# Sliding-window attention and SwiGLU on one core: the last third of the output weights queued ahead of the second tile's values, the fourth tile's values loaded one attention step later

## The chip, the cores and the metric

The kernel runs on one core of a Trainium2 chip. The metric is the device time of one execution in microseconds (us), lower is better. Three executions of the kernel before took 330.44, 330.54 and 331.67 us, median 330.54.

## The reference, cut to what matters

```python
# q, k, v: (8 batches, 8 heads, 576 positions, 64); window = 64
scores = (q @ k.T) / sqrt(64)                  # per batch and head
mask   = (0 <= i - j) & (i - j < 64)           # causal, 64 wide
attn   = softmax(where(mask, scores, -1e9)) @ v
x      = attn, heads side by side               # (4608 tokens, 512)
out    = (silu(x @ w_gate) * (x @ w_val)) @ w_out   # 512 -> 1536 -> 512
```

All inputs and the output are float32; the kernel computes in bfloat16 with float32 sums.

## The kernel before, in words

The 4608 tokens are worked through as nine tiles of 512 tokens, `t` = 0 to 8. Tiles 0 to 6 and 8 are the first 512 positions of one batch each; tile 7 (`LAST`) gathers the last 64 positions of all eight batches. Counted from one, "the second tile" is t = 1 and "the fourth tile" is t = 3.

Each tile passes three stages on TensorE (PE):

- **attention**: `scores` (L261), an exponential on ScalarE (ACT), a mask product and a sum on VectorE (DVE, L277 and L282), `totals` (L294), and `mix`, the product with the values (L347). DVE scales the result into `xT` (L359).
- **gate and value**: `gate_value` (L398 to L405) for each of twelve blocks `m` of 128 of the 1536 inner columns: four matmuls with `wg`, four with `wv` (all L401), a SiLU on ACT (L394), and a product on DVE into `hT` (L395). PE's two kinds of result tile, `g_ps` and `v_ps`, have two buffers each, so block m + 2 can't start on its value tile before DVE has read that of block m.
- **projection**: `project` and `project_part` (L410), twelve matmuls with `wo` for each of four row groups of the tile; `project_end` copies a row group to `os_` and SyncE (SP) writes it out (L420, L429).

The order on every engine is written out by hand (`manual_schedule`); each engine works through its own instructions in order and waits on semaphores. The projection of tile t - 1 is laid between the attention steps of tile t (L652 to L666), then the gate blocks of tile t follow (L682). In the first round this is the prologue L638 to L650: `scores(1, ...)`, and `columns(c0, c1)`, which projects tile 0 column by column: `columns(7, 10)` uses columns 7, 8 and 9 of `wo`, and `mix_all(1)` comes right after it.

While the gate blocks run, DVE also turns the queries and keys of the next tile (`turn`, L198 and L208), after blocks 4, 6, 8, 10 for t = 1 and 1, 4, 7, 10 later (L681).

**The loads.** GpSimd (POOL) issues the loads that change float32 to bfloat16 on the way: the weights `wg`, `wv`, `wo`, the queries `q_s` (four transfers for a tile, L88), the keys `k_s` (sixteen, L108), and the values of tiles 1 and 2, which go straight into `vb[1]` and `vb[0]` (`load_halves`, eight transfers, one for each head, L137). `wo` comes in three transfers of four columns each (`weights_o`, L178): columns 0 to 3, 4 to 7, 8 to 11. Each transfer that POOL issues signals one of eight semaphores in turn, and an issue waits until the transfer eight places before it has landed. So POOL never has more than eight in flight.

From t = 3 on the values go another way. `stage_v(t)` (L155) has SP load them as float32 into `v_f`, a tile with one buffer, in eight transfers (L137); `cast_v(t)` (L159) has POOL change them to bfloat16 in `vb[t % 2]` with four CASTs (L162). In round t the order is `cast_v(t + 1)`, `load_qk(t + 2)`, `stage_v(t + 2)` (L667 to L675); in round 1 `cast_v` is left out. So in the kernel before the values of tile 3 are staged in round 1, behind the four writes of tile 0's output on SP, and cast in round 2. POOL's CASTs and its DMA issues stand in one order: what is queued behind a waiting CAST waits with it. In round 2 these are the loads of q and k of tile 4, and of `k_l` (L677, sixteen transfers for tile 7).

The two places that the change touches are L561 to L565 (the order of `wo` and `vb[1]` on POOL) and L672 to L675 (the place of `stage_v(3)` on SP).

Of the kernel before, what the change touches and what calls it, by code (L numbers as in the profile page):

```python
# [17 lines left out]
def kernel(  # L18
# [15 lines left out]
    LAST = NT - 2  # L34
# [27 lines left out]
    def batch(t):  # L62
        return t if t < LAST else t - 1
# [38 lines left out]
    def load_k(k_s, groups):  # L102

        w = 4 * D - 32
        for a, c in quarters:
            p0 = 64 * a + 32 * c
            for g, (b, s) in enumerate(groups):
                nc.gpsimd.dma_start(  # L108
                    k_s[p0:p0 + 32, g, :, 0:w],
                    k[b, a:H:2, s:s + P].rearrange("u (r e) d -> r u (e d)", e=4)  # L110
                    [:, :, 32 * c:32 * c + w],
                )
        return k_s

    def load_qk(t):
        q_s = load_q(t)
        if t == 1:
            staged[t] = q_s, None
            return
        if t == LAST:  # L120
            groups = [(b, S - P) for b in range(4)]
        else:
            groups = [(batch(t), P * g) for g in range(4)]
        k_s = stage.tile([P, 4, 4, 4 * D], BF16, name="k_s", tag="k")
        staged[t] = q_s, load_k(k_s, groups)
# [7 lines left out]
    def load_halves(eng, dst, t):  # L133

        for hd in range(H):
            w, x, h = hd // 4, hd // 2 % 2, hd % 2
            eng.dma_start(  # L137
                dst[64 * x:64 * x + 64, :, w, h],
                v[batch(t), hd, 0:512].rearrange("(j r) d -> r j d", r=64),
            )  # L140

    def load_last_v():
        for c in range(2):
            for hd in range(H):
                w, x, h = hd // 4, hd // 2 % 2, hd % 2
                s0 = S - P + 64 * c
                nc.gpsimd.dma_start(
                    vl[64 * x:64 * x + 64, :, c, w, h],
                    v[:, hd, s0:s0 + 64].rearrange("b r d -> r b d"),
                )  # L150

    def new_v(t):
        staged[t, "v"] = stage.tile([P, 8, 2, 2, D], FP32, name="v_f", tag="v", bufs=1)

    def stage_v(t):  # L155
        new_v(t)
        load_halves(nc.sync, staged[t, "v"], t)

    def cast_v(t):  # L159
        for i in range(4):  # L160
            js = slice(2 * i, 2 * i + 2)
            nc.gpsimd.tensor_copy(vb[t % 2][:, js], staged[t, "v"][:, js])  # L162
# [14 lines left out]
    def weights_o(c0, c1):  # L177
        nc.gpsimd.dma_start(  # L178
            wo[:, c0:c1, :],
            moe_w_out[P * c0:P * c1].rearrange("(c r) f -> r c f", r=P),  # L180
        )
# [21 lines left out]
    def turn(t, u):  # L203
        turn_q(t, u)
        turn_k(kT[t % 2], staged[t][1], u)

    def turn_k(dst, k_s, u):
        nc.vector.transpose(  # L208
            dst[:, u, :].rearrange("r (g x e) -> r g e x", g=4, e=4),
            k_s[:, :, u].rearrange("r g (e d) -> r g e d", d=D)[:, :, :, 0:32],  # L210
        )
# [97 lines left out]
    def sums(t, w):  # L309
        d = d_tile(), d_tile()  # L310
        totals(t, w, d)
        for x in range(2):
            r = room(1)[:, 0]
            log(r, d[x])
            invert(r)
            inverse[t, 2 * w + x] = r
# [54 lines left out]
    def mix_all(t):  # L371
        tiles = wide("ao_ps"), wide("ao_ps")
        for w in range(2):
            mix(t, w, (tiles[w][:, 0], tiles[w][:, 1]))
        for u in range(4):
            scale(t, u, tiles[u // 2][:, u % 2])
# [20 lines left out]
    def gate_value(t, m):  # L397
        pair = gate_tiles()  # L398
        for ps, w in zip(pair, (wg, wv)):
            for c in range(4):  # L400
                nc.tensor.matmul(  # L401
                    ps[:], w[:, c, P * m:P * m + P], xT[t][:, c, :],
                    start=(c == 0), stop=(c == 3),
                )
        gate_end(t, m, pair)  # L405

    def project_part(t, ss, tiles, cs):
        for c in cs:
            for s, o_ps in zip(ss, tiles):
                nc.tensor.matmul(  # L410
                    o_ps[:], hT[t][:, c, P * s:P * s + P], wo[:, c, :],
                    start=(c == 0), stop=(c == 11),
                )

    def project_end(t, s, o_ps, copy=nc.vector.tensor_copy):
        os_ = fsb.tile([P, 512], FP32, name="os_", tag="os_", bufs=4)
        copy(os_[:], o_ps[:])
        rows = out[S * batch(t):S * batch(t) + 512]
        if t < TURNED:
            nc.sync.dma_start(rows.rearrange("(r e) f -> e r f", e=4)[s], os_[:])  # L420
            return
        if t == LAST:
            rows = out.rearrange("(b s) f -> b s f", s=S)[:, 512:S]
            rows = rows.rearrange("b (r e) f -> e b r f", e=16)
        else:
            rows = rows.rearrange("(r e) f -> e r f", e=16)
        for i in range(4):
            eng = nc.scalar if t == NT - 1 and i % 2 else nc.sync
            eng.dma_start(rows[4 * s + i], os_[32 * i:32 * i + 32])  # L429

    def out_tile():
        return ps_f.tile([P, 512], FP32, name="o_ps", tag="g")

    def project(t, s):
        o_ps = out_tile()
        project_part(t, (s,), (o_ps,), range(12))
        project_end(t, s, o_ps)
# [17 lines left out]
    def set_exp():  # L455
        nc.scalar.preload_act_table_set("natural_log_exp_and_others")  # L456

    def set_silu():
        nc.scalar.preload_act_table_set("silu_and_others")
# [101 lines left out]
    load_qk(1)  # L561
    weights_o(0, 4)
    weights_o(4, 8)
    load_halves(nc.gpsimd, vb[1], 1)
    weights_o(8, 12)  # L565
    for i in range(2):
        on_v(v1[:, i], v_first[:, i])
    scores_first(2)
# [83 lines left out]
    for t in range(1, NT):  # L652
        if t > 1:
            set_exp()
            scores(t, 0)
            project(t - 1, 0)
            o_ps = out_tile()
            project_part(t - 1, (1,), (o_ps,), range(5))
            scores(t, 1)
            sums(t, 0)  # L660
            project_part(t - 1, (1,), (o_ps,), range(5, 12))
            project_end(t - 1, 1, o_ps)
            project(t - 1, 2)
            sums(t, 1)
            mix_all(t)
            project(t - 1, 3)  # L666
        set_silu()  # L667
        if t + 1 == LAST:
            load_last_v()
        elif t + 1 < NT and t > 1:  # L670
            cast_v(t + 1)
        if t + 2 < NT:  # L672
            load_qk(t + 2)
            if t + 2 != LAST:
                stage_v(t + 2)  # L675
        if t == 2:
            k_l = load_k(  # L677
                cast.tile([P, 4, 4, 4 * D], BF16, name="k_l", tag="c0"),
                [(b, S - P) for b in range(4, 8)],
            )  # L680
        turns = (4, 6, 8, 10) if t == 1 else (1, 4, 7, 10)  # L681
        for m in range(12):  # L682
            gate_value(t, m)
            if m in turns and t + 1 < NT:
                turn(t + 1, turns.index(m))
            if m == 8 and 3 <= t < 7:
                turn_k(kT[2], k_l, t - 3)
# [32 lines left out]
```

## Time and profile before

| what | value |
|---|---|
| median of three executions | 330.54 us |
| the profiled execution's own time | 330.49 us |
| its span, first to last instruction | 328.5 us, so 2.0 us lie around the span |
| mean granted TensorE clock | 0.997 |
| PE busy | 319.1 us, 97% of the span |
| DVE, ACT, POOL busy | 220.7, 167.1, 143.5 us |
| POOL's DMA queue | 57.3% of 16 engines over the span |
| SP's DMA queue | 18.7% of 16 engines over the span |

The times in the views are us from the start of the span unless marked ns. A line of the timeline gives start, duration, engine, source line, operation, the tiles written and read, and how many instructions are merged in it; in brackets stands the idle time of the engine before it and what ended that time. A matmul's duration overlaps the next one's, so the time that PE loses at a wait is read from start to start. The view of DMA issues, asked for a stretch that holds one issue, gives the time from that issue to its landing; it has this for POOL's transfers and not for SP's.

### The profile page before, as it was taken

The numbers are of one execution on the slowest core, as the hardware profiler recorded it, in microseconds if no ns is written. First come the engines' busy times: TensorE is split into PE (matmuls) and PEld (weight loads), VectorE is DVE, ScalarE is ACT, GpSimd is POOL, SyncE is SP. The second block draws the span as 40 slices with busy tenths as digits, with TensorE's granted clock in tenths as the row PEclk, the third lists the DMA queues.
The fourth block names the chain that finished last, engine by engine and source line by source line (L and its number), as shares of the span: only waits on it lengthen the run. The fifth ranks groups of instructions, "written<-read, shape, count | busy, mean of one in ns | idle before, by whom it ended". The sixth has DMA issues, their size and how long they took to land.

```text
span 328.5 us, 7003 instructions
## 1 busy us (share of the span) xinstructions
PE 319.1 (97%) x2743; PEld 151.3 (46%) x2743; DVE 220.7 (67%) x352; ACT 167.1 (51%) x239; POOL 143.5 (44%) x256
## 2 busy tenths in 40 slices
PE   7899999989999999999999999999999999999995
PEld 4444434434444444445444544444444544444443
DVE  4865755497857776787668766976787576773431
ACT  4854556336833583357435653566347633773300
POOL 4953465778857935246123899464200000000000
PEclk9999999999999999999999999999999999999998
DMA  7999999999899799329821999899401300020013
GB/s 250 201 201 201 204 148 208 231 199 131 141 238 184 88 208 185 68 42 216 173 65 16 145 190 98 57 177 198 110 3 34 98 0 2 12 87 32 2 34 96
DMA packets 82865, 40.84 MB, mean 124 GB/s; under 512 B 64272, under 2 KB 78352, under 8 KB 82832
## 3 DMA queue, kind: packets, MB, share of 16 engines
q0 software_dynamic: 50672, 23.08, 57.3%
q1 hardware_dynamic: 31136, 16.26, 18.7%
q10 hardware_dynamic: 1024, 1.05, 1.1%
q8 instruction: 21, 0.34, 0.4%
q14 instruction: 12, 0.10, 0.1%
HBM read 54.00 MB, written 9.44 MB: 193 GB/s over the span
## 4 chain that ended last, share of the span: by engine, by line
PE 85%; DMA 8%; DVE 2%; issue 2%; ACT 1%; POOL 1%; SPq 0%; DVEq 0%; POOLq 0%
PE g_ps L401 26%; PE v_ps L401 26%; PE o_ps L410 25%; DMA k_s<-in_k_dram 3%; DMA q_s<-in_q_dram 2%; PE s_ps L261 2%; DMA v_f<-in_v_dram 2%; PE ao_ps L347 2%; PE d_ps L294 1%; DMA k_f<-in_k_dram 1%; PE o_ps L446 1%; PE g_ps L381 1%; PE v_ps L381 1%; ACT L456 0%; PE ao_ps L330 0%
## 5 line engine op out<-in xcount | busy, mean ns | idle before, releaser
L394 ACT ACTIVATE sg<-g_ps 128x512 f32<-128x512 f32 x108 | 64.4, 597 | 115.1 <-PE g_ps L401 87.5
L395 DVE TENSOR_TENSOR hT<-sg,v_ps 128x512 bf16<-128x512 f32 x108 | 74.6, 692 | 59.4 <-PE v_ps L401 57.1
L401 PE MATMUL v_ps<-xT,wv 128*128 128x512 bf16 x424 | 108.8, 379 | 1.0 <-DVE hT L395 1.0
L401 PE MATMUL g_ps<-xT,wg 128*128 128x512 bf16 x424 | 108.8, 379 | 0.1
L410 PE MATMUL o_ps<-wo,hT 128*128 128x512 bf16 x420 | 95.3, 380 | 0.8 <-DMA wo<-in_moe_w_out_dram 0.8
L108 POOL DMA_DIRECT2D k_s<-in_k_dram x112 | 60.4, 551 | 25.0 <-DMA q_s<-in_q_dram 14.8
L401 PEld LDWEIGHTS <-wv 128*128 128x128 bf16 x424 | 41.5, 98 | 51.2 <-issue 1.3
L401 PEld LDWEIGHTS <-wg 128*128 128x128 bf16 x424 | 41.3, 98 | 49.5 <-issue 0.6
L410 PEld LDWEIGHTS <-hT 128*128 128x128 bf16 x420 | 39.1, 98 | 47.5 <-issue 2.9
L274 ACT ACTIVATE eb<-s_ps 128x960 bf16<-128x960 f32 (+1 forms) x32 | 29.5, 974 | 16.3 <-PE s_ps L261 16.2
L208 DVE STREAM_TRANSPOSE kT<-k_s 128x512 bf16<-128x512 bf16 x28 | 35.9, 1284 | 2.0 <-issue 2.0
L277 DVE TENSOR_TENSOR eb<-eb,mask 128x960 bf16<-128x960 bf16 (+1 forms) x32 | 21.6, 675 | 14.3 <-ACT eb L274 14.2
L359 DVE TENSOR_TENSOR xT<-ao_ps,r 128x512 bf16<-128x512 f32 x36 | 23.0, 685 | 7.2 <-PE ao_ps L347 5.6
L162 POOL CAST vb<-v_f 128x512 bf16<-128x512 f32 x20 | 11.9, 644 | 29.7 <-DMA v_f<-in_v_dram 21.6
L304 ACT ACTIVATE r<-d_ps 128x512 f32<-128x512 f32 (+1 forms) x33 | 20.8, 629 | 6.0 <-PE d_ps L294 5.9
L198 DVE STREAM_TRANSPOSE qT<-q_s 128x512 bf16<-128x512 bf16 x32 | 22.4, 702 | 0.6 <-DMA q_s<-in_q_dram 0.6
L307 ACT ACTIVATE r<-r 128x512 f32<-128x512 f32 (+1 forms) x33 | 22.0, 669 | 1.0
L88 POOL DMA_DIRECT2D q_s<-in_q_dram x28 | 15.2, 551 | 16.4 <-DVE qT L198 10.2
L282 DVE TENSOR_TENSOR both<-eb 128x512 bf16<-128x512 bf16 x32 | 13.9, 434 | 1.1
L137 POOL DMA_DIRECT2D vb<-in_v_dram x16 | 10.9, 689 | 7.9 <-DMA wo<-in_moe_w_out_dram 3.8
L456 ACT ACT_TABLE_LOAD x9 | 11.5, 1283 | 2.0 <-issue 1.9
L95 POOL DMA_DIRECT2D q_s<-in_q_dram x16 | 8.6, 598 | 7.8 <-DVE qT L198 6.8
(107 smaller groups left out, 186.8 us busy)
## 6 DMA issues: line engine op xcount, KB each, us to landing
q_s<-in_q_dram POOLq DMA_DIRECT2D x28, 248.0 KB, 6.3
k_s<-in_k_dram POOLq DMA_DIRECT2D x112, 56.0 KB, 4.5
v_f<-in_v_dram SPq DMA_DIRECT2D x40, 128.0 KB
wo<-in_moe_w_out_dram POOLq DMA_DIRECT2D x3, 512.0 KB, 11.1
q_f<-in_q_dram SPq DMA_DIRECT2D x4, 256.0 KB
vb<-in_v_dram POOLq DMA_DIRECT2D x16, 64.0 KB, 5.7
v<-in_v_dram POOLq DMA_DIRECT2D x16, 64.0 KB, 3.1
q_s<-in_q_dram POOLq DMA_DIRECT2D x16, 62.0 KB, 4.0
```

Source lines behind the costliest of these rows:

```text
L108: nc.gpsimd.dma_start(k_s[p0:p0 + 32, g, :, 0:w], k[b, a:H:2, s:s + P].rearrange("u (r e) d -> r u (e d)", e=4) [:, :, 32 * c:32 * c + w],)
L198: nc.vector.transpose(queries[t][:, u, :].rearrange("r (e x) -> r e x", e=16), staged[t][0][:, u].rearrange("r (e d) -> r e d", d=D)[:, :, ...
L208: nc.vector.transpose(dst[:, u, :].rearrange("r (g x e) -> r g e x", g=4, e=4), k_s[:, :, u].rearrange("r g (e d) -> r g e d", d=D)[:, :, ...
L274: nc.scalar.activation(flat, s_ps[h][:].rearrange("r a b -> r (a b)")[:, 0:n], AF.Exp, scale=0.125)
L277: nc.vector.tensor_mul(flat, flat, mask[:].rearrange("r j c e y -> r (j c e y)")[:, 0:n])
L304: nc.scalar.activation(r, d_ps, AF.Ln)
L307: nc.scalar.activation(r, r, AF.Exp, scale=-1.0)
L359: nc.vector.tensor_mul(xT[t][:, u, :], o_ps, inverse.pop((t, u)))
L394: nc.scalar.activation(sg[:], g_ps[:], AF.Silu)
L395: nc.vector.tensor_mul(hT[t][:, m, :], sg[:], v_ps[:])
L401: nc.tensor.matmul(ps[:], w[:, c, P * m:P * m + P], xT[t][:, c, :], start=(c == 0), stop=(c == 3),)
L410: nc.tensor.matmul(o_ps[:], hT[t][:, c, P * s:P * s + P], wo[:, c, :], start=(c == 0), stop=(c == 11),)
```

## The change

Two moves; nothing is added and nothing is taken away. The third transfer of `wo` is issued by POOL ahead of the eight transfers of `vb[1]`, not behind them. The eight transfers of `stage_v(3)` are issued by SP in round 2, after the write of row group 0 of tile 1's output, and no longer in round 1 behind tile 0's output.

```diff
     load_qk(1)
     weights_o(0, 4)
     weights_o(4, 8)
+    weights_o(8, 12)
     load_halves(nc.gpsimd, vb[1], 1)
-    weights_o(8, 12)
     for i in range(2):
         on_v(v1[:, i], v_first[:, i])
...
             set_exp()
             scores(t, 0)
             project(t - 1, 0)
+            if t == 2:
+                stage_v(3)
             o_ps = out_tile()
             project_part(t - 1, (1,), (o_ps,), range(5))
...
         if t + 2 < NT:
             load_qk(t + 2)
-            if t + 2 != LAST:
+            if t > 1 and t + 2 != LAST:
                 stage_v(t + 2)
```

On PE, DVE, ACT the order of instructions stays as it was. On POOL one transfer changes its place among nine; on SP the eight transfers of `v_f` move behind the four writes of `os_` of row group 0 of tile 1.

## The prediction

> **What bounds the kernel now.** I read the page first: engine shares, and in its groups the idle time before each matmul.
>
> ```profile
> PE 319.1 (97%) x2743; PEld 151.3 (46%) x2743; DVE 220.7 (67%) x352; ACT 167.1 (51%) x239; POOL 143.5 (44%) x256
> ...
> L401 PE MATMUL v_ps<-xT,wv 128*128 128x512 bf16 x424 | 108.8, 379 | 1.0 <-DVE hT L395 1.0
> ...
> L410 PE MATMUL o_ps<-wo,hT 128*128 128x512 bf16 x420 | 95.3, 380 | 0.8 <-DMA wo<-in_moe_w_out_dram 0.8
> ```
>
> PE is the bound, and once the pipeline is full the big matmuls wait twice, once each: for `wo` and for `hT`. PE's timeline says where and how long.
>
> ```profile
> 47.72 1.04 PE L410 MATMUL o_ps<-wo,hT 128*128 128x512 bf16 x4
> 49.56 1.89 PE L410 MATMUL o_ps<-wo,hT 128*128 128x512 bf16 x8 [0.80 <-DMA wo<-in_moe_w_out_dram]
> 51.37 1.04 PE L347 MATMUL ao_ps<-eb,vb 64*64 64x128 bf16 x64
> ...
> 66.35 1.03 PE L401 MATMUL g_ps<-xT,wg 128*128 128x512 bf16 x4
> 68.38 1.02 PE L401 MATMUL v_ps<-xT,wv 128*128 128x512 bf16 x4 [1.00 <-DVE hT L395]
> ```
>
> The bracket understates the loss, because a matmul's duration overlaps the next one's. Four matmuls take 1.04 us and one 0.38, so they start (1.04 - 0.38) / 3 = 0.22 us apart. After the four at 47.72 the next was due at 47.72 + 4 x 0.216 = 48.59; it came at 49.56, **0.97 us** late. After the four at 66.35 the next was due at 67.22; it came at 68.38, **1.16 us** late. The table of stretches, cut from gate start to gate start, confirms the second (columns: stretch, its length, then busy time of each engine).
>
> ```profile
> 54.27:89.33 35.06, 34.06 (x281) 15.89 (x281) 25.74 (x38) 19.27 (x28) 29.15 (x51) 1.00 1.22 180
> 89.33:123.22 33.89, 33.89 (x281) 15.86 (x280) 24.19 (x36) 17.97 (x27) 22.98 (x43) 1.00 1.14 180
> ```
>
> The round with the wait is 35.06 - 33.89 = 1.17 us longer than the next, which PE fills wholly. So 0.97 + 1.16 = 2.13 us can be had, no more: the later rounds have no wait to take.
>
> What ends the two waits is read from the timelines of POOL, SP and DVE.
>
> ```profile
> 31.41 0.70 POOL L137 DMA_DIRECT2D vb<-in_v_dram  x1 [0.57 <-DMA wg<-in_moe_w_gate_dram]
> ...
> 42.80 0.68 POOL L137 DMA_DIRECT2D vb<-in_v_dram  x1 [1.98 <-DMA wo<-in_moe_w_out_dram]
> 43.47 0.77 POOL L178 DMA_DIRECT2D wo<-in_moe_w_out_dram  x1
> ...
> 60.55 0.55 POOL L108 DMA_DIRECT2D k_s<-in_k_dram  x1 [0.73 <-DMA k_s<-in_k_dram]
> ```
>
> ```profile
> 57.15 7.68 SPq L137 DMA_DIRECT2D v_f<-in_v_dram  x8
> ```
>
> ```profile
> 66.50 1.31 DVE L208 STREAM_TRANSPOSE kT<-k_s 128x512 bf16<-128x512 bf16 x1 [2.02 <-issue]
> ```
>
> The third `wo` is issued last, at 43.47, and the DMA view for that issue says 6.0 us to landing: 49.51, and PE goes on at 49.56. The sixteenth `k_s` of tile 2 is issued at 60.55 and lands 5.8 us later, at 66.32; DVE, which wants it for `kT`, had nothing to do since 64.47 and starts at 66.50. Its 1.31 us delay the `hT` of block 5, which PE needs to reuse a `v_ps` buffer. SP's eight `v_f` transfers run from 57.15 to 64.83, exactly beside those keys.
>
> **Part one, `wo` ahead of `vb[1]`.** Nothing is added, nine transfers change order. POOL's transfers land in the order of issue: the view gives 11.1 and 12.4 us for the first two `wo` (issued 28.73 and 30.09: landed 39.86 and 42.52), then the eight `vb[1]` 0.3 to 0.6 us apart until 45.97. In the new order the third `wo` takes the slot at 31.41 and stands right behind the second; two `wo` landed 42.52 - 39.86 = 2.66 us apart, so it lands at about 42.52 + 2.66 = 45.2. PE wants it at 48.59: the wait goes, 3.4 us to spare. Saved: 0.97.
>
> What is late next? The `vb[1]`, which `mix` would now read from 51.37 - 0.97 = 50.40. Each issue moves one slot back. The eighth waits for the transfer eight before it, now the third `wo`: it is issued at 45.2 + 0.28 (as 42.52 led to 42.80) = 45.5, and lands 3.2 us later by the row of the eighth `vb[1]` before (42.80 to 45.97): 48.7. It holds head 7, wanted by the second half of `mix`, half of its 1.0 us later, at 50.9. That is 2.2 us to spare. The median of all sixteen `vb` on the page, 5.7, would give 51.2, a wait of 0.3; the worst row, 11.5 us (the first `vb[1]`, issued behind two `wo`), would give 57.0, a wait of 6.1. I take 3.2, because its neighbours ahead in the queue are the same small transfers; the 11.5 had 2 `wo` and earlier loads before it. So part one is worth 0.97, bounds 0.97 - 6.1 = -5.1 and 0.97.
>
> The Trainium skill, page "DMA: Bandwidth & Descriptors", section "Anatomy of one DMA — SWDGE (gpsimd) path", fits a transfer from GpSimd as about 2.0 us plus its bytes over 436 GB/s. For the 64 KB of one `vb` that estimate is 2.15 us, where the row has 3.2; by the page the eighth would land at 47.6, and the sum stays the same.
>
> The other thing ready just then: `mix` needs the second `ao_ps` buffer, free when ACT's second logarithm (49.25, 1.00 us) ends at 50.25, before 50.9; so 0.6 us are left there. POOL's q and k issues of tile 2 start at 45.5 + 0.7 = 46.2 and not 44.22. By landing this costs nothing: before, the third `wo` stood ahead of them until 49.51. The first `q_s` was behind it and landed at 50.71; now it takes 46.2 + 4.1 (the quickest row of a first `q_s`, 111.62 to 115.70, but for one of 3.9) = 50.3.
>
> **Part two, `v_f` of tile 3 later.** Without `v_f`, what do the last `k_s` of tile 2 cost? The nearest row is tile 3's: nine `k_s` issued from 76.34, with nothing of SP beside them, take 2.3 us to landing (view of DMA issues, median), against 4.6 to 6.1 for the last ten of tile 2. SP's four writes of tile 0's output stay (54.24 to 57.05, moving 0.97 earlier with PE). The fifteenth and sixteenth issues wait for the seventh and eighth to land (before 59.00 and 60.27). I take these about 1 us earlier, since half of what delayed them was those writes, so the sixteenth is issued near 59.5 and lands after 2.3 to 4.0 us, at 61.8 to 63.5. DVE would want it at 64.47 - 0.97 = 63.5. And DVE has room: `hT` of block 5 ended at 68.34 and cost PE 1.16 us, so `kT` might have started at 66.50 - 1.16 = 65.34 with no loss, 64.4 on the new clock. Even issued at 60.55 as before, the sixteenth would be there with up to 3.8 us to landing. So the wait goes: 1.16 saved. Bounds: 0, if SP's writes and POOL's own pace hold the keys, and 1.16.
>
> What the move adds: SP reads its row-group write first (81.17, 1.75 us, on the new clock 79.0 to 80.8), then eight issues of 6.3 to 7.7 us, until about 88, landing about 90. Behind them on SP stand the writes of row groups 1 to 3 (85.81 to 94.2 before), some 2 to 4 us late. Nobody waits: `os_` has four buffers, and the next copy into the first comes at 114.36. `cast_v(3)`, before at 81.15 with no wait, now waits until about 90. Behind it on POOL stand q and k of tile 4 and `k_l`, 15.3 + 10.3 us of issues, and `cast_v(4)`. They shift from 83.84 to about 92.7, 9 us, so that the last `k_s` of tile 4, landed 103.89 before, lands near 113. DVE turns it at 128.18 - 2.1 = 126.1: 13 us to spare. `cast_v(4)` moves from 109.39 to about 118, needed by `mix` of tile 4 near 151. `cast_v(3)` itself, done near 92.7, is needed at 119.67 - 2.1 = 117.6. `v_f` of tile 4 waits on the only buffer, free at 92.7; on SP it started at 94.26 before, so it does not move.
>
> The CASTs also meet other work of DVE. At 81.15 they met L277, and one took 1.19 us, not 0.65; that round still lost nothing but the 1.16. At 109.39 (2.27 us) one met `qT` at 109.19 (0.70) and `kT` at 109.82 (1.29), both as long as anywhere. So I put the new meetings at 0, up to 0.5.
>
> A rule against this part: "DMA: Bandwidth & Descriptors", section "Rules for kernel authors", says to issue a DMA early, compute, and wait late. By it `v_f` stays at 57.15, 24 us ahead of its CAST, and the sum keeps the 1.16: 329.5 us. The trace shows what early costs here, so I follow the row.
>
> **Sum.** 330.49 - 0.97 - 1.16 = **328.4 us** for an execution like the profiled one (span 326.4); that one was 0.05 under the median of 330.54. It is 0.6% faster; a measurement of this kernel can tell about 0.5%, here 1.65 us or a time under 328.9, from no change.
>
> **Rivals.**
>
> (a) *The keys stay late.* SP's writes of tile 0 and the eight-in-flight limit set the landing, not `v_f`. For: the sixth `k_s` landed 1.6 us behind the fifth, at 57.63, when `v_f` had hardly begun. Against: those after SP's writes were through stayed at 4.9 to 6.1 us to landing. Only part one counts: 330.49 - 0.97 = 329.5. Half of the wait left: 328.9.
>
> (b) *The values take the place of the weights.* At 5.7 us to landing `mix` waits 0.3: 328.7; if they land only as late as the third `wo` makes the tail of this queue, about 51.9, part one is worth nothing: 329.3. Both (a) and this: 330.5, no change.
>
> (c) *Slower.* The eighth `vb[1]` takes the 11.5 us of the first one before, queued behind bulk: PE waits 6.1 us at `mix`, 330.49 - 2.13 + 6.1 = 334.5. It costs from 3.2 + 2.2 = 5.4 us to landing on, and makes the kernel slower than before from 7.5. Against: the eighth cannot be issued before the third `wo` has landed, so no bulk stands before it.
>
> **Chances.** Forecast 0.70 (328.4, from 327.9 to 328.9: 0.5 below for waits too small to have a row, 0.5 above for the CASTs). (a) 0.14, (b) alone 0.07, both 0.04, (c) 0.05. The range from 327.9 to 329.6 holds the forecast, (a) and (b). Faster by over 0.5%: 0.70; within: 0.24, from (a), (b), both; slower: 0.06, (c) and what I have not seen.
>
> **What would show it.** No wait on `wo` before L410 near 48.6; `mix` starting near 50.4 with no wait on `vb`; POOL's `wo` at 31.4. No idle of DVE before the first `kT` of tile 2, near 63.5, and no wait on `hT` before `v_ps`; that round 33.9 us long. `cast_v(3)` waiting for `v_f` until about 90, and later rounds still 33.9. I am wrong if `mix` waits for `vb`, if `kT` still waits for `k_s`, or if a round after the second grows.

## The result, and the profile after

The changed kernel takes 328.43 us (median of four executions, 328.10 to 328.69) against 331.06 for the kernel before beside it: a ratio of **0.992**, 95% interval 0.9893 to 0.9947. Run again later it took 328.23 (five executions) against 330.66 (seventeen): 0.9923, 0.9907 to 0.9939. The forecast was 328.4, range 327.9 to 329.6, faster by over 0.5%.

The profiled execution takes 328.23 us, its span is 326.2. The page has lost both waits that bounded PE: the groups of L401 and L410 name neither `hT` nor `wo` any more. (Some matmul records are missing here, so the counts and PE's busy time are lower than the work.)

```profile
PE 315.9 (97%) x2700; PEld 150.7 (46%) x2743; DVE 220.2 (67%) x352; ACT 167.2 (51%) x239; POOL 142.8 (44%) x256
...
L401 PE MATMUL v_ps<-xT,wv 128*128 128x512 bf16 x415 | 107.2, 379 | 0.1
L410 PE MATMUL o_ps<-wo,hT 128*128 128x512 bf16 x396 | 93.6, 380 | 1.5 <-issue 0.3
```

PE's timeline at the two places: the twelve matmuls of columns 7 to 9 run through from 47.65, `mix` follows at 50.34, and the groups of four gate and value matmuls follow one another every 0.86 us.

```profile
47.65 2.76 PE L410 MATMUL o_ps<-wo,hT 128*128 128x512 bf16 x12
50.34 1.04 PE L347 MATMUL ao_ps<-eb,vb 64*64 64x128 bf16 x64
...
64.46 1.03 PE L401 MATMUL v_ps<-xT,wv 128*128 128x512 bf16 x4
65.32 1.03 PE L401 MATMUL g_ps<-xT,wg 128*128 128x512 bf16 x4
66.18 1.03 PE L401 MATMUL v_ps<-xT,wv 128*128 128x512 bf16 x4
```

The stretches from gate start to gate start: the round that was 35.06 us long is now as long as the next ones.

```profile
53.24:87.13 33.89, 33.63 (x276) 15.89 (x281) 25.14 (x38) 19.26 (x28) 21.62 (x38) 1.00 1.13 163
87.13:121.02 33.89, 33.63 (x276) 15.86 (x280) 24.20 (x36) 17.97 (x27) 25.37 (x48) 1.00 1.06 169
```

POOL, SP and DVE, in this order:

```profile
31.30 0.74 POOL L178 DMA_DIRECT2D wo<-in_moe_w_out_dram  x1 [0.56 <-DMA wg<-in_moe_w_gate_dram]
...
45.54 0.68 POOL L137 DMA_DIRECT2D vb<-in_v_dram  x1 [2.24 <-DMA vb<-in_v_dram]
46.27 2.16 POOL L88 DMA_DIRECT2D q_s<-in_q_dram  x4
...
60.55 0.55 POOL L108 DMA_DIRECT2D k_s<-in_k_dram  x1 [0.42 <-DMA k_s<-in_k_dram]
...
90.19 2.29 POOL L162 CAST vb<-v_f 128x512 bf16<-128x512 f32 x4 [9.79 <-DMA out_dram<-os__1234]
```

```profile
80.78 6.79 SPq L137 DMA_DIRECT2D v_f<-in_v_dram  x8
```

```profile
63.71 1.32 DVE L208 STREAM_TRANSPOSE kT<-k_s 128x512 bf16<-128x512 bf16 x1 [0.27 <-issue]
```

The third `wo` goes out at 31.30 and lands at 45.25. The eighth `vb[1]` goes out at 45.54 and lands 2.8 us later, at 48.34, 2 us before `mix`. The sixteenth `k_s` goes out at 60.55, as before, but lands in 3.0 us and not in 5.8: DVE stands idle for 0.27 us before it, which PE doesn't feel. `v_f` runs at 80.78 and its CAST at 90.19. (POOL's long wait there is put down to a write of `os_`; by the kernel that CAST waits for the eight `v_f`.)

**The ledger.** The last group of matmuls (L446) starts at 321.71 before and at 319.51 after, 2.20 us earlier. The prologue's gate start was 0.23 us earlier by itself (20.81 to 20.58), but PE gave 0.16 of it back waiting for the queries of tile 1, so that `columns(0, 4)` begins 0.07 earlier (39.97 to 39.90). From there to `mix` (51.37 to 50.34) another 0.96 is gained, and in the round of tile 1 1.17: 0.07 + 0.96 + 1.17 = 2.20.

### The profile page after: what moved, and what is told of

The parts are those of the page before. It is cut to its first block, busy times and chain, and to the rows that moved or that the text cites. A ratio compares the mean times of both kernels' runs of the same rounds, so it can differ in the third digit from the quotient of the medians.

```text
span 326.2 us, 6959 instructions
## 1 busy us (share of the span) xinstructions
PE 315.9 (97%) x2700; PEld 150.7 (46%) x2743; DVE 220.2 (67%) x352; ACT 167.2 (51%) x239; POOL 142.8 (44%) x256
## 4 chain that ended last, share of the span: by engine, by line
PE 86%; DMA 8%; POOL 3%; issue 1%; DVE 1%; SPq 0%; DVEq 0%; POOLq 0%
PE o_ps L410 28%; PE g_ps L401 26%; PE v_ps L401 25%; DMA wv<-in_moe_w_val_dram 4%; DMA q_s<-in_q_dram 3%; PE s_ps L261 3%; PE ao_ps L347 2%; PE d_ps L294 1%; DMA q_f<-in_q_dram 1%; POOL wg L172 1%; POOL wv L172 1%; PE o_ps L446 1%; POOL v L129 1%; POOL qk_b L517 0%; DVE qT L198 0%
## 5 line engine op out<-in xcount | busy, mean ns | idle before, releaser
L401 PE MATMUL g_ps<-xT,wg 128*128 128x512 bf16 x415 | 108.2, 379 | 0.9
L401 PE MATMUL v_ps<-xT,wv 128*128 128x512 bf16 x415 | 107.2, 379 | 0.1
L410 PE MATMUL o_ps<-wo,hT 128*128 128x512 bf16 x396 | 93.6, 380 | 1.5 <-issue 0.3
L401 PEld LDWEIGHTS <-wv 128*128 128x128 bf16 x424 | 41.5, 98 | 50.1
L401 PEld LDWEIGHTS <-wg 128*128 128x128 bf16 x424 | 41.3, 98 | 49.5 <-issue 0.6
L410 PEld LDWEIGHTS <-hT 128*128 128x128 bf16 x420 | 39.1, 98 | 46.5 <-issue 1.8
```

The source lines that it names most:

```text
L401: nc.tensor.matmul(ps[:], w[:, c, P * m:P * m + P], xT[t][:, c, :], start=(c == 0), stop=(c == 3),)
L410: nc.tensor.matmul(o_ps[:], hT[t][:, c, P * s:P * s + P], wo[:, c, :], start=(c == 0), stop=(c == 11),)
```

## The experiments

The experiments were compared with the kernel before on the same chip (median 330.7 to 330.8 us); the row "changed" has 331.06 beside it, as above. The table has, from one profiled execution of each kernel, three stretches of PE between the first weight loads of successive gate stages (for the first tile that is L381, the part of its gate stage in the prologue). Without any wait the second is 34.08 and the third 33.89; the first holds the wait for `wo`, and varies by some tenths with the wait for the queries of tile 1 at its middle (and in vf_only by 0.28 in the prologue).

| kernel | median, us | ratio, 95% interval | gate 0 to 1 | gate 1 to 2 | gate 2 to 3 |
|---|---|---|---|---|---|
| before | 330.7 to 330.8 | | 38.11 | 35.25 | 33.89 |
| changed | 328.43 | 0.992 (0.9893 to 0.9947) | 37.31 | 34.08 | 33.89 |
| wo_only | 331.43 | 1.0026 (0.9996 to 1.0056) | 37.19 | 37.39 | 33.89 |
| vf_only | 329.41 | 0.9945 (0.9924 to 0.9967) | 38.49 | 34.08 | 33.89 |
| vf_half_early | 330.65 | 0.9991 (0.9973 to 1.0009) | 37.69 | 36.20 | 34.33 |
| vf_after_keys | 329.59 | 0.9956 (0.9936 to 0.9976) | 37.40 | 34.08 | 35.24 |
| wo_middle_vf_early | 330.14 | 0.9979 (0.9962 to 0.9997) | 37.51 | 34.38 | 34.98 |
| wo_middle_vf_late | 328.62 | 0.993 (0.9912 to 0.9949) | 37.66 | 34.08 | 33.89 |
| cast_moved | 328.56 | 0.9929 (0.9912 to 0.9946) | 37.17 | 34.08 | 33.89 |
| values_behind_q | 330.80 | 1.0009 (0.9991 to 1.0027) | 39.67 | 34.08 | 33.89 |
| before_casts_moved | 330.30 | 0.998 (0.9965 to 0.9995) | 38.65 | 34.14 | 33.89 |
| wo_middle_casts_moved | 328.96 | 0.9944 (0.9926 to 0.9961) | 37.33 | 34.20 | 33.89 |
| changed_again | 328.23 | 0.9923 (0.9907 to 0.9939) | 37.50 | 34.08 | 33.89 |

**wo_only: part one alone.**

```diff
     weights_o(4, 8)
+    weights_o(8, 12)
     load_halves(nc.gpsimd, vb[1], 1)
-    weights_o(8, 12)
```

> Part one alone: the third transfer of the output weights goes ahead of the second tile's values, the values of tile 3 stay in round 1. My theory: the wait on the weights (0.96 us) goes and the wait on the keys of tile 2 (1.17 us) stays, so about 1.0 us less than the kernel before, 329.5 where before has 330.5; the round of the second tile stays 35.06 us long. Rival 'the values take the place of the weights': PE waits for the last values at the mix of tile 1, nothing gained, 330.5. Rival 'both parts lean on each other' (the keys come earlier once the queue ahead of them is reordered): the keys' wait shrinks too, 328.4 to 329.0.

None of the three came. The wait for the weights is gone (the first stretch), but the wait for the keys is nearly three times as long, and the kernel no faster; its executions scatter from 330.21 to 335.21 us. PE, DVE and POOL of this kernel:

```profile
65.38 1.03 PE L401 MATMUL g_ps<-xT,wg 128*128 128x512 bf16 x4
69.30 1.02 PE L401 MATMUL v_ps<-xT,wv 128*128 128x512 bf16 x4 [2.89 <-DVE hT L395]
```

```profile
67.42 1.31 DVE L208 STREAM_TRANSPOSE kT<-k_s 128x512 bf16<-128x512 bf16 x1 [3.91 <-DMA vb<-in_v_dram]
```

```profile
46.20 2.16 POOL L88 DMA_DIRECT2D q_s<-in_q_dram  x4
...
61.44 1.08 POOL L108 DMA_DIRECT2D k_s<-in_k_dram  x2 [1.17 <-DMA k_s<-in_k_dram]
```

The `v_ps` due at 65.38 + 4 x 0.216 = 66.25 came at 69.30, 3.05 us late, where it was 1.16 in the kernel before. The keys landed at 67.24; DVE's wait is put down to a `vb`, which shares its semaphore.

The wait is 1.89 us longer, and that has two parts. PE comes to the keys 0.97 us earlier, since it no longer waits for the weights; the keys do not come earlier with it, so by this alone the 0.97 us gained at the weights are lost again at the keys. And the keys landed 0.92 us later than before (67.24 against 66.32). POOL could not issue the eighth value before the third `wo` had landed, so q and k of tile 2 began at 46.20 and not at 44.22, and the sixteenth key went out at 61.98 and not at 60.55. SP's writes and `v_f` also came 0.93 us earlier with PE (56.22); wo_middle_vf_early, below, speaks against this as the cause. Another 0.25 us went at `mix` of tile 2, behind a mask product that took 1.75 us (83.14), for a reason that vf_after_keys shows. The sum, 0.97 gained and 1.89 + 0.25 lost, is what the last group of matmuls shows: it starts at 322.88, 1.17 us later than before.

**vf_only: part two alone** (the changed kernel with the order of `wo` and `vb[1]` of before).

> Part two alone: the values of tile 3 are loaded in round 2, the weights stay behind the second tile's values. My theory: the wait on the keys (1.17 us) goes, that on the weights (0.96 us) stays: 329.3 where before has 330.5, the round of the second tile 33.9 us long. Rival 'the writes of tile 0 and the eight in flight hold the keys': the wait on the keys stays and the time is that of before, 330.5.

As my theory had it: the wait on the keys is gone, that for the weights is there (1.01 us), 329.41. Rival (a) of the prediction falls: with SP's writes and the eight-in-flight limit in place, taking `v_f` away is enough.

**vf_half_early: half of tile 3's values beside the keys.**

```diff
+            if t == 1:
+                new_v(3)
+                load_halves(nc.sync, staged[3, "v"], 3, range(4))
...
             if t == 2:
-                stage_v(3)
+                load_halves(nc.sync, staged[3, "v"], 3, range(4, 8))
```

> As the changed kernel, but the values of tile 3 are split: heads 0 to 3 are loaded in round 1, where the kernel before had all eight, and heads 4 to 7 in round 2. Everything is still computed. My theory is that the bytes beside the last keys make them late: in the changed kernel the sixteenth key transfer landed at 63.5 with 0.7 us left before PE would feel it, with all eight values it was 3 us later on the same clock and cost 1.17. Half the bytes should bring it about 1.5 us later, to 65, a wait of PE of about 0.6 us: 329.0. Rival 'the mere presence of a second queue': as with all eight, 329.5. Rival 'the writes of tile 0': no difference from the changed kernel, 328.4.

The direction was right and the size was not: the round is 2.12 us longer, not 0.6. Measured from the gate start (53.24, 53.67 and 53.30), the sixteenth key landed at 10.3 us with no `v_f`, 13.0 with four transfers, 13.9 with eight. But from its own issue to its landing it took 3.0, 5.8 and 5.3 us. Four transfers held up this key as much as eight, so its lateness doesn't go by the bytes, and the rival 'the mere presence of a second queue' is not excluded for it. What eight do more lies in the issue of that key, 7.3, 7.2 and 8.7 us behind the gate start. Each of these is one execution. (0.44 us more went in the third stretch, for a reason that the next experiment shows: a mask product at 116.48 took 1.93 us.)

**vf_after_keys: `v_f` in round 1, but behind the keys.**

```diff
+            if t == 1 and m == 4:
+                new_v(3)
+                nc.vector.memset(staged[3, "v"][0:64, 0, 0, 0, 0:1], 0.0)
+                load_halves(nc.sync, staged[3, "v"], 3)
...
-            if t == 2:
-                stage_v(3)
```

> As the changed kernel, but the values of tile 3 are loaded in round 1 after all, held back until the keys of tile 2 are read: DVE writes one column of the values' tile behind the first turn of the keys (gate block 4), and the transfers wait for it, so that they start near 65 and not at 57. My theory: what costs is the overlap with the keys alone, so the time is that of the changed kernel, 328.4 (0.05 us more on DVE, hidden), the cast is ready at its old place near 80, and the transfers beside the values of tile 2 and the q and k of tile 3 do no harm, since these have 10 us or more in hand. Rival 'any 1 MB on the other queue in round 1 makes some later load late': a new wait, most likely on the first turn of tile 3 or the mix of tile 2, 328.9 to 329.6.

On the keys the theory held: the same 1 MB, from 64.5 on, costs the round of tile 1 nothing. But a new wait came, in a place that no theory had named: the third stretch is 1.35 us longer. POOL, DVE and PE there:

```profile
109.77 2.71 POOL L162 CAST vb<-v_f 128x512 bf16<-128x512 f32 x4
```

```profile
109.90 2.12 DVE L277 TENSOR_TENSOR eb<-eb,mask 128x960 bf16<-128x960 bf16 x1 [0.67 <-ACT eb L274]
112.05 0.71 DVE L282 TENSOR_TENSOR both<-eb 128x512 bf16<-128x512 bf16 x1
```

```profile
112.82 0.40 PE L294 MATMUL d_ps<-both,ones 64*64 64x512 bf16 x2
113.84 0.40 PE L294 MATMUL d_ps<-both,ones 64*64 64x512 bf16 x2 [0.62 <-DVE both L282]
```

`cast_v(4)` started 0.13 us ahead of the mask product; the product took 2.12 us and not 0.65, and PE waited at the sums. In the changed kernel this CAST comes at 117.19, behind the last mask product, because POOL had waited for `v_f` until 90.19.

**cast_moved: the same, with this one CAST behind the loads of q and k.**

```diff
-        elif t + 1 < NT and t > 1:
+        elif t + 1 < NT and t > 1 and t != 3:
             cast_v(t + 1)
         if t + 2 < NT:
             load_qk(t + 2)
+            if t == 3:
+                cast_v(t + 1)
```

> As the kernel with the values of tile 3 held back behind the first turn of the keys, which ran at 329.6: its first two waits were gone, but in round 3 DVE's mask product at 109.9 took 2.12 us and not 0.65, while POOL's cast of tile 4's values ran from 109.77, and PE lost 0.3 and 0.8 us at the sums. Here this one cast is put behind the loads of q and k of tile 5, so that it no longer stands beside that product. Theory 'the cast and the mask product block each other': the product takes 0.65 us again, no wait at the sums, 328.4 to 328.6. Rival 'the loads beside it did that': the product stays long, 329.5. Risk: the values of tile 5 start later by the same 16 us and are cast late, at most in the round of tile 5.

The CAST runs at 126.86, the product at the same place takes 0.66 us, and the third stretch is 33.89 again: 328.56.

```profile
109.89 0.66 DVE L277 TENSOR_TENSOR eb<-eb,mask 128x960 bf16<-128x960 bf16 x1 [0.67 <-ACT eb L274]
```

**wo_middle_vf_early and wo_middle_vf_late: the third `wo` in the middle of the values.** The first keeps `v_f` in round 1, the second has it in round 2 like the changed kernel.

```diff
     weights_o(4, 8)
-    load_halves(nc.gpsimd, vb[1], 1)
+    load_halves(nc.gpsimd, vb[1], 1, range(4))
     weights_o(8, 12)
+    load_halves(nc.gpsimd, vb[1], 1, range(4, 8))
```

> The third transfer of the output weights in the middle of the second tile's values (after heads 0 to 3), the values of tile 3 in round 1 as before. With the weights ahead of all eight values and tile 3's values in round 1 the wait on the weights went, but the wait on the keys grew from 1.17 to 3.05 us. Theory 'eight in flight': there the eighth value had to wait for the third weights to land, so all issues of q and k of tile 2 began at 46.2 and not at 44.2, and this pushed the keys 2 us further into the traffic of tile 3's values. In the middle, the transfer that waits for the third weights is the fourth q, near 47, and what stands before it is issued as in the kernel before: the keys' wait is then 1.2 us or less and the weights (landing near 47) are there by 48.6: 329.3 to 329.5 where before has 330.5. Rival 'SP's traffic comes 0.96 us earlier with PE while POOL's doesn't': the keys' wait stays over 2 us, 330.5 to 331.5.

> The same place of the weights, the values of tile 3 in round 2 as in the changed kernel. Theory 'eight in flight': no wait on weights, values or keys; PE cannot gain more than the changed kernel has, so 328.4, but the sixteenth key transfer lands 1 to 2 us earlier than its 63.5, which leaves about 2 us and not 0.7 before PE would feel it. Rival: the place makes no difference to the keys, 63.5 again. Risk: the weights land after 48.6 and up to 0.5 us come back.

On the waits for weights and keys the theory held for both. POOL and SP of the first:

```profile
44.20 1.66 POOL L88 DMA_DIRECT2D q_s<-in_q_dram  x3
47.12 0.55 POOL L88 DMA_DIRECT2D q_s<-in_q_dram  x1 [1.26 <-DMA wo<-in_moe_w_out_dram]
```

```profile
55.62 9.55 SPq L137 DMA_DIRECT2D v_f<-in_v_dram  x8
```

Three queries go out from 44.20, as before the change; only the fourth waits for the third `wo`. The keys' wait is 0.30 us, not 3.05, and no wait for the weights is left. The rival falls: `v_f` starts at 55.62 here, earlier still than the 56.22 of wo_only, and the keys' wait is small. The time is 330.14 and not the 329.3 to 329.5 expected: the third stretch is 1.09 us longer, lost at the sums of tile 3, where `cast_v(4)` met the mask products once more (110.61 and 110.62). (The 0.76 us in the expectation of wo_middle_casts_moved is this loss, counted too low.) In the second the sixteenth key landed 9.3 us behind the gate start (63.15 - 53.85), against 10.3 in the changed kernel. That is 1.0 us more in hand, and PE gains nothing from it: 328.62.

**values_behind_q: the values behind other transfers, close to the prediction's slower rival.**

```diff
     weights_o(8, 12)
+    q_s2 = load_q(2)
     load_halves(nc.gpsimd, vb[1], 1)
```

> As the changed kernel, but the four query transfers of tile 2 go ahead of the second tile's values: this is the rival of the prediction in which the values come late, made on purpose. Theory 'transfers of POOL land in the order of issue': weights at 45.2, queries until about 50.2 at 1.25 us each, then the values at 50.6 to 53.7, where the mix of tile 1 asks for the first half at 50.3 and the second at 50.8. PE waits some 1.7 us for head 3 and 1.2 more for head 7, in all about 2.9: 331.3 where before has 330.5. If values are not bound to the order, they land by 48.3 and the time is 328.4.

The values landed between 50.19 and 53.24, each in its turn, and `mix` waited in four places:

```profile
51.13 0.24 PE L347 MATMUL ao_ps<-eb,vb 64*64 64x128 bf16 x2 [0.34 <-DMA vb<-in_v_dram]
51.56 0.64 PE L347 MATMUL ao_ps<-eb,vb 64*64 64x128 bf16 x30 [0.19 <-DMA vb<-in_v_dram]
52.86 0.24 PE L347 MATMUL ao_ps<-eb,vb 64*64 64x128 bf16 x2 [0.65 <-DMA vb<-in_v_dram]
53.28 0.60 PE L347 MATMUL ao_ps<-eb,vb 64*64 64x128 bf16 x29 [0.18 <-DMA vb<-in_v_dram]
```

The stretch is 2.4 us longer than in the changed kernel and the time 2.4 us more, for an expected 2.9. A transfer lands by its place in POOL's queue, as the prediction had it.

**before_casts_moved, wo_middle_casts_moved, changed_again.** The first two move `cast_v(3)` and `cast_v(4)` behind the loads of q and k in their rounds, in the kernel before and in wo_middle_vf_early.

```diff
-        elif t + 1 < NT and t > 1:
+        elif t + 1 < NT and t > 3:
             cast_v(t + 1)
         if t + 2 < NT:
             load_qk(t + 2)
+            if t in (2, 3):
+                cast_v(t + 1)
```

> The kernel before with one edit: the casts of tile 3's and tile 4's values stand behind the loads of q and k in their rounds, so that they fall into the gate blocks (near 99 and 127) and no longer beside the mask products (82 to 84, 112 to 115). The two waits that the change is about (0.96 and 1.17 us) stay. Theory 'part of the measured gain is the casts': the kernel before runs from 329.7 to 332.3, and its slow executions are those in which a cast meets a mask product; here the median is 0.3 to 0.5 us lower, near 330.3, and no execution is over 331. Rival 'the spread comes from the loads of the prologue': median and spread as before.

> The third transfer of the weights in the middle of the second tile's values, tile 3's values in round 1 as in the kernel before, and the same two casts behind the loads of q and k. With the weights in the middle the keys' wait was 0.30 us, and 0.76 us more were lost at the sums of tile 3 where a cast met a mask product, median 330.1. Theory: with the casts out of the way 0.3 us of the keys' wait is all that is left over the changed kernel, 328.7 to 328.9. So nearly the whole gain is to be had without part two. Rival 'tile 3's values beside the keys cost more than this look showed': 329.3 or more, with a keys' wait near 1 us.

> The changed kernel, unaltered, beside the other two on one chip: 328.4, spread under 1 us since neither cast of tiles 3 and 4 stands beside a mask product.

The casts are worth 0.36 us of median to the kernel before (330.66 to 330.30, ratio 0.998, 0.9965 to 0.9995). Its spread is not explained by them: it still ran from 329.12 to 331.12. In its profiled execution the wait for the weights was 1.28 us and that for the keys 0.07:

```profile
47.71 1.04 PE L410 MATMUL o_ps<-wo,hT 128*128 128x512 bf16 x4
49.87 1.89 PE L410 MATMUL o_ps<-wo,hT 128*128 128x512 bf16 x8 [1.12 <-DMA wo<-in_moe_w_out_dram]
...
66.66 1.03 PE L401 MATMUL g_ps<-xT,wg 128*128 128x512 bf16 x4
67.59 1.02 PE L401 MATMUL v_ps<-xT,wv 128*128 128x512 bf16 x4
```

Up to there this kernel is the kernel before, so both waits vary from one execution to the next. Part of it is the same see-saw as in wo_only: PE came to the keys 0.31 us later, and they had landed 0.8 us earlier. wo_middle_casts_moved came at 328.96, just above the 328.9 expected, with 0.12 us of the keys' wait left. So most of the change's gain is to be had with `v_f` where it was, if the weights hold up nothing on POOL and the casts keep clear of the mask products. changed_again has 328.23 and a spread of 0.63 us, as expected. None of these versions beats the changed kernel: in the stretches of the table PE has, besides a wait of 0.60 us in the prologue (18.66, for `xT`), only the wait for the queries of tile 1 left, and none of these edits is aimed at either.

## Why the prediction was right

- **Which waits go, and their size: right.** 0.97 and 1.16 were read from start to start; 0.96 and 1.17 were gained.
- **The values do not take the weights' place: right.** Third `wo` at 45.2, eighth value issued at 45.5, landed at 48.7, said the prediction; 45.25, 45.54 and 48.34 it was. The Trainium skill's estimate of 2.15 us for such a transfer (page "DMA: Bandwidth & Descriptors", section "Anatomy of one DMA — SWDGE (gpsimd) path") stands against 2.8 measured; it would have misled by too little to matter. Rivals (b) and (c) did not come; with the values behind the queries (values_behind_q) the time is 2.4 us longer, for 2.9 expected from the queue's order.
- **The time of the sixteenth key: wrong by 1 us.** I had its issue at 59.5, earlier by half of what SP's writes were thought to cost; it stayed at 60.55, and in vf_only, with POOL's old order, it was 60.36. So neither the move of `v_f` nor the earlier writes brought it forward. It landed at 63.53, the last moment of the interval (61.8 to 63.5), and of the room behind it 0.7 us was left.
- **The later issues of q and k "by landing cost nothing": right for the first q, nearly so for the keys without `v_f`, wrong with it.** The first q landed at 50.71 in both kernels. The sixteenth key landed about 0.3 us later in the changed kernel than in vf_only (63.53 against 63.3), and 0.92 later in wo_only than before.
- **The sum of two parts, each with its own price: right in total, wrong in its terms.** Under rival (a) I gave 329.5 for part one alone; it measured 331.43 against 330.77 before, no gain at all. The step that was wrong: where the keys stay late, PE reaches them 0.97 us earlier and waits 0.97 us longer, so by my own numbers part one alone was worth nothing, 330.5. Part two alone gives 1.4 us of median, both give 2.4 to 2.6. The sum held since it was made from two waits that both end in the changed kernel, not from the worth of each part by itself.
- **What `v_f` does to the keys: right.** Rival (a), at 14%, is excluded by vf_only and vf_after_keys. In the table the seven profiles without `v_f` beside the keys all have 34.08 in the second stretch, the six with it 34.14 to 37.39. The half dose confirms it in kind, not in proportion, and the size is not fixed: the same prologue cost 1.17 us in one execution and 0.07 in another (before and before_casts_moved).
- **The chain behind `cast_v(3)`: right.** CAST expected at about 90, `cast_v(4)` at about 118, the last key of tile 4 at about 113; measured 90.19, 117.19 and 111.47, with nobody waiting.
- **"New meetings" of the CASTs at 0, up to 0.5: right for the changed kernel, too cheap as a bound.** A meeting cost up to 1.35 us (vf_after_keys). I had judged from one row in which the product ran 1.19 us and PE had cover. The Trainium skill, page "SBUF — State Buffer", section "Who interferes with whom", has the rule that I did not use: a DVE instruction with two SBUF inputs contends with a GpSimd instruction that reads SBUF, one with at most one such input (outside its two-port modes) doesn't. The traces agree: the mask product (two inputs in SBUF) went to 1.06 to 2.12 us beside a CAST, and in these profiles it took longer than 0.70 us only there, while `hT` (one input in PSUM) and the turns of q and k kept theirs (0.69, 0.70, 1.29).
- **The measured gain is a little more than the forecast's 2.13.** Medians differ by 2.4 to 2.6 us. The forecast was made against one execution, at 330.49 a little under the kernel's medians (330.66 to 331.06); of the rest, up to 0.36 us can be the casts (before_casts_moved). How much of that figure the changed kernel gains was not measured by itself. That 328.4 was met within 0.03 us is luck in part: the two waits were read from a single execution, and they vary.
- **The rule to issue a DMA early and to wait for it late** (page "DMA: Bandwidth & Descriptors", section "Rules for kernel authors") spoke for 329.5. It would have been wrong here: the same transfers, issued 24 us later or only 7 us later, free the keys.

## What to carry to other kernels

Price a reordering of loads by the whole queue behind it: with a fixed number of transfers in flight, a large one put ahead holds up the issue of what comes that many places later, and what it costs shows at another consumer. A load without a deadline belongs behind one that has one, also when it goes by another queue. And before adding up the gains at two waits that follow each other, ask what ends the second: if it ends by a load's landing, an engine that comes earlier only waits longer, and the first gain is there only once the second wait is gone too. An experiment with each edit alone says it at once.

## What I had not expected of the hardware

Four CASTs on GpSimd and a product with two SBUF inputs on VectorE that run at the same time stretch each other: the product from 0.65 to between 1.06 and 2.12 us, the CASTs from 2.29 to between 2.71 and 3.37 us.

In the rows that I compared, the seventh key of tile 2 went out within 0.05 us of the landing of the fourth query (54.36 and 54.37 before, 54.60 and 54.61 after, 53.31 and 53.32 in wo_middle_vf_early), about 1.2 us after the third query, whose semaphore it waits for. The profile names no cause and no run tells it apart. Also open, and not tried: the prologue's gate start varies from 20.3 to 20.9 us in these profiles, and PE waits up to 0.7 us for the queries of tile 1 near 39.4.
